# Longer load runs for q and k, 64x64 transposes and disjoint output views in an attention kernel followed by routed experts

## The chip, the cores and the metric

The kernel runs on one core of one Trainium2 chip. The metric is the device time of one execution in microseconds (us); lower is better. Before the change the median was 398.99 us (398.04 to 399.03, 3 runs). A ratio in this text is the mean time of one kernel's fast runs over the mean of the other's fast runs of the same rounds, so it is not quite the ratio of the medians quoted beside it; in the experiments the profiled execution is left out of it. A run over 1.5% above the fastest of its kernel counts as slow, and differences are read from fast runs.

## The reference

```python
# q, k, v: (8 batches, 8 heads, 576 positions, 64), float32
scores = q @ k^T / 8, blocks of 64 positions, causal by block   # row block i sees column blocks <= i
attn   = softmax(scores); x = (attn @ v) laid out as 4608 tokens x 512
# domain_id: one of 8 experts for each token; w1 (8,512,1024), w2 (8,1024,512)
for e in range(8):
    mask = domain_id == e
    out[mask] = relu(x[mask] @ w1[e]) @ w2[e]
```

A *pair* below is two heads of one batch; there are 32 pairs, four to a batch. The *routing* turns the domain ids into lists of token numbers, five blocks of 128 tokens for each expert. The experts gather their tokens' rows of x from DRAM, multiply twice, and scatter the rows of the result.

## The kernel before: the parts concerned

q, k and v come as rows of 64 elements. GpSimd's queue (POOL) casts them to 16 bit on the way, apart from batch 0, which is cast by the engines (all code below is cut and simplified):

```python
def load_sw(dst, src, t, b0, b1):            # two batches
    for c in range(5):
        nc.gpsimd.dma_start(
            out=dst[t % 2][0:n, c, o0:o1, 0:D],
            in_=src[b0:b1, :, 128*c : 128*c + n, :].rearrange("b h p d -> p (b h) d"))
```

For each pair, TensorE transposes q and k (ten transposes of 128x128), VectorE (DVE) copies them out of PSUM in one instruction, TensorE makes the scores, ScalarE (ACT) the exponentials, TensorE the product with v, and DVE normalises. The tile vS holds v in 16 bit; VE holds parts of it laid out for two heads at once, and DVE copies it from vS once a batch. One step of the routing stands between each two pairs:

```python
for p in range(npair + 1):
    emit_G(0, st)                                  # scores, first third
    if p + 2 < npair: QKs[p + 2] = emit_T(p + 2)   # transposes two pairs ahead
    emit_G(1, st); emit_P(prev); emit_G(2, st); emit_Q(prev)
    ...
    next(rout, None)                               # a step of the routing
```

The routing finds the token of each slot with 36 accumulating matmuls of one-hot tiles (`lhsT=L[:, j, :], rhs=Hh[:, :, j, :]`). In the experts every output block goes out by a scatter into one and the same tensor:

```python
osb = msb.tile([128, DM], F32, name="osb", tag="osb", bufs=4)
nc.vector.tensor_copy(out=osb[:], in_=po[:])
nc.gpsimd.indirect_dma_start(
    out=out, out_offset=bass.IndirectOffsetOnAxis(ap=tok[:, blk : blk + 1], axis=0),
    in_=osb[:], in_offset=None, bounds_check=N - 1, oob_is_err=False)
```

The softmax here doesn't subtract the row's maximum and nothing guards it: scores larger than these inputs give would overflow.

Of the kernel before, what the change touches and what calls it, by code (L numbers as in the profile page):

```python
# [8 lines left out]
F32 = mybir.dt.float32  # L9
F16 = mybir.dt.float16  # L10
# [7 lines left out]
def kernel(  # L18
# [19 lines left out]
    HP = H // 2  # L38

    ctx.enter_context(tc.manual_schedule())  # L40
    xd = nc.dram_tensor("x_rows", (N, DM), F16, kind="Internal").ap()

# [7 lines left out]
    qS = [asb.tile([128, 5, 16, D], F16, name=f"qS{i}") for i in range(2)]  # L50
    kS = [asb.tile([128, 5, 16, D], F16, name=f"kS{i}") for i in range(2)]
    vS = [asb.tile([128, 5, 16, 66], F16, name=f"vS{i}") for i in range(2)]
    VE = [asb.tile([128, 5, HP, 132], F16, name=f"VE{i}") for i in range(2)]
    ATE = [asb.tile([128, 832], F16, name=f"ATE{i}") for i in range(3)]


    def stage(nm):
        return asb.tile([128, 5, H, D], F32, name=nm, tag="stg", bufs=3)

    qf, kf, vf = stage("qf"), stage("kf"), stage("vf")  # L60
    dom_i = const.tile([128, 2 * NJ], I32, name="dom_i")

    def load_pair0(eng, dst, src):
        for h in range(2):
            eng.dma_start(
                out=dst[:, 0:4, h, :],
                in_=src[0, h, 0:512, :].rearrange("(c p) d -> p c d", p=128))
        eng.dma_start(
            out=dst[0:64, 4, 0:2, :],
            in_=src[0, 0:2, 512:576, :].rearrange("h p d -> p h d"))  # L70

    def load_rest(eng, dst, src, h0):
        for c in range(5):
            n = min(128, S - 128 * c)
            eng.dma_start(
                out=dst[0:n, c, h0:H, :],
                in_=src[0, h0:H, 128 * c : 128 * c + n, :].rearrange("h p d -> p h d"))

    load_pair0(nc.sync, qf, q)
    load_pair0(nc.scalar, kf, k)  # L80
# [3 lines left out]
    load_rest(nc.sync, qf, q, 2)  # L84
    load_rest(nc.scalar, kf, k, 2)
    load_rest(nc.sync, vf, v, 0)

    identh = const.tile([128, 128], F16, name="identh")
    make_identity(nc, identh[:])
    up = const.tile([128, 128], F16, name="up")  # L90
# [7 lines left out]
    def load_sw(dst, src, t, b0, b1):  # L98
        o0 = 8 * (b0 - 2 * t)
        o1 = o0 + 8 * (b1 - b0)  # L100
        for c in range(5):
            n = min(128, S - 128 * c)
            nc.gpsimd.dma_start(  # L103
                out=dst[t % 2][0:n, c, o0:o1, 0:D],
                in_=src[b0:b1, :, 128 * c : 128 * c + n, :].rearrange(
                    "b h p d -> p (b h) d"))

    def load_weights(w1_e, w2_e):
        w1h = wsb.tile([128, 4, Fdim], F16, name="w1h", tag="w1h", bufs=3)
        nc.gpsimd.dma_start(  # L110
            out=w1h[:], in_=w1_e.rearrange("(c p) f -> p c f", p=128))
        w2h = wsb.tile([128, 8, DM], F16, name="w2h", tag="w2h", bufs=3)
        nc.gpsimd.dma_start(
            out=w2h[:], in_=w2_e.rearrange("(c p) f -> p c f", p=128))
        return w1h, w2h

    for src, dst in ((q, qS), (k, kS), (v, vS)):
        load_sw(dst, src, 0, 1, 2)
# [5 lines left out]
    lo_f = const.tile([128, NJ], F32, name="lo_f")  # L124
# [3 lines left out]
    tok0 = const.tile([128, E * NB], I32, name="tok0")  # L128
    xg = [const.tile([128, NB, DM], F16, name=f"xg{i}") for i in range(2)]
    for i in range(2):  # L130
        nc.vector.memset(qS[i][64:128, 4], 0.0)
        nc.vector.memset(kS[i][64:128, 4], 0.0)
    nc.vector.memset(vS[0][:, :, :, 64:66], 1.0)
    for i in range(3):
        nc.vector.memset(ATE[i][:, 0:64], 1.0)
        nc.vector.memset(ATE[i][:, 64:832], 0.0)
    nc.vector.memset(VE[0][:], 0.0)

    def cast(fn, dst, src, h0, h1):
        fn(out=dst[:, 0:4, h0:h1, 0:D], in_=src[:, 0:4, h0:h1, :])  # L140
        fn(out=dst[0:64, 4, h0:h1, 0:D], in_=src[0:64, 4, h0:h1, :])

    cast(nc.vector.tensor_copy, qS[0], qf, 0, 2)
    cast(nc.scalar.copy, kS[0], kf, 0, 2)


    def onehot(L, Hh, ub, ncols, base):
        nc.vector.tensor_scalar(
            out=ub, in0=u_f[:], scalar1=base, scalar2=None, op0=ALU.subtract)
        yield  # L150
        nc.vector.tensor_tensor(
            out=Hh[:, 0], in0=iota_h[:, 0:ncols].unsqueeze(1).to_broadcast([128, NJ, ncols]),
            in1=ub.unsqueeze(2).to_broadcast([128, NJ, ncols]), op=ALU.is_equal)
        yield
        nc.vector.tensor_scalar(
            out=Hh[:, 1], in0=Hh[:, 0], scalar1=p_f[:, 0:1], scalar2=None, op0=ALU.mult)
        nc.vector.tensor_tensor(
            out=Hh[:, 2], in0=Hh[:, 0],
            in1=iota_h[:, 0:NJ].unsqueeze(2).to_broadcast([128, NJ, ncols]), op=ALU.mult)
        yield  # L160
        for j in range(NJ):
            nc.vector.tensor_scalar(
                out=L[:, j, :], in0=iota_h[:], scalar1=lo_f[:, j : j + 1],
                scalar2=None, op0=ALU.is_equal)
            if j % 4 == 3:
                yield


    def inverse(ps, L, Hh, ncols, inv, tok):
        for j in range(NJ):  # L170
            nc.tensor.matmul(
                out=ps[:, 0 : 3 * ncols].rearrange("p (a c) -> p a c", a=3),
                lhsT=L[:, j, :], rhs=Hh[:, :, j, :],
                start=(j == 0), stop=(j == NJ - 1))
        nc.vector.tensor_copy(
            out=inv, in_=ps[:, 0 : 3 * ncols].rearrange("p (a c) -> p a c", a=3))
        nc.vector.tensor_scalar(
            out=inv[:, 0], in0=inv[:, 0], scalar1=-1.0e6, scalar2=1.0e6,
            op0=ALU.mult, op1=ALU.add)
        nc.vector.tensor_tensor(out=inv[:, 1], in0=inv[:, 1], in1=inv[:, 2], op=ALU.add)  # L180
        nc.vector.tensor_tensor(out=tok, in0=inv[:, 0], in1=inv[:, 1], op=ALU.add)

    def slot_col(r_f, d_f, w, u, nm):
# [18 lines left out]
    def routing():  # L202
        nc.vector.tensor_copy(out=iota_h[:], in_=iota_i[:])
# [13 lines left out]
        ps_t = aps.tile([128, 512], F32, name="poP", tag="poP")  # L217
        ps_r = aps.tile([128, 512], F32, name="poQ", tag="poQ")
# [14 lines left out]
        cnt = asb.tile([128, E], F32, name="cnt")  # L233
# [8 lines left out]
        ri = slot_col(rank[:], dom_f[:], NJ, u_f[:], "t")  # L242
# [3 lines left out]
        nc.vector.tensor_copy(out=lo_f[:], in_=lo_i[:])  # L246
        yield

        ul = asb.tile([128, E], F32, name="ul")
        slot_col(cnt[:], iota_h[:, 0:E], E, ul[:], "e")  # L250
        yield
        um = asb.tile([128, 1], F32, name="um")
        nc.vector.tensor_reduce(out=um[:], in_=ul[:], axis=AX.X, op=ALU.max)
        umi = asb.tile([128, 1], I32, name="umi")
        nc.vector.tensor_scalar(
            out=umi[:], in0=um[:], scalar1=-float(NB * (E - 1)), scalar2=205.0,
            op0=ALU.add, op1=ALU.mult)
        nc.vector.tensor_scalar(out=n_i[:], in0=umi[0:1, :], scalar1=10, scalar2=None,
                                op0=ALU.arith_shift_right)
        nc.vector.memset(base_f[:], 0.0)  # L260
        yield
        L = asb.tile([128, NJ, 128], F16, name="L", tag="stg", bufs=3)
        Hh = asb.tile([128, 3, NJ, E * NB], F16, name="Hh", tag="stg", bufs=3)
        ub = asb.tile([128, NJ], F16, name="ub")
        yield from onehot(L, Hh, ub[:], E * NB, base_f[:, 0:1])
        ps = aps.tile([128, 512], F32, name="poP", tag="poP")
        inv = asb.tile([128, 3, E * NB], F32, name="inv")
        inverse(ps, L, Hh, E * NB, inv[:], tok0[:])
        yield
        for i in range(2):  # L270
            nc.vector.memset(xg[i][:], 0.0)
            yield


    def emit_T(p):
        b, hp = divmod(p, HP)
        t = b // 2
        PT = aps.tile([128, 2, 1024], F16, name="PT", tag="PT")
        QK = asb.tile([128, 2, 576], F16, name="QK", tag="QK", bufs=3)
        h0 = 8 * (b % 2) + 2 * hp  # L280
        for s, src in enumerate((qS[t % 2], kS[t % 2])):
            for c in range(5):
                nc.tensor.transpose(  # L283
                    out=PT[:, s, 128 * c : 128 * c + 128],
                    in_=src[:, c, h0 : h0 + 2, :].rearrange("p h d -> p (h d)"),
                    identity=identh[:])
        nc.vector.tensor_copy(out=QK[:], in_=PT[:, :, 0:576])  # L287
        return QK

# [284 lines left out]
```

## Time and profile before

| stage of the profiled run | from, to (us) | length |
|---|---|---|
| attention, to the end of the last normalisation | 0 to 161.8 | 161.8 |
| stores of x, gathers, to the first transpose of an expert | 161.8 to 169.2 | 7.4 |
| experts, to the end of TensorE's last matmul | 169.2 to 371.9 | 202.7 |
| tail, to the end | 371.9 to 398.3 | 26.4 |

The four add up to the span, so each question about the change can be put to one stage. The prediction shows the lines that say what binds each: slow loads and a late start in attention, scatters that wait for one another in the experts. Two more groups of instructions are wanted later (line, engine, operation, output and input, shapes and count, then busy us and mean ns of one):

```profile
L287 DVE COPY QK<-PT 128x1152 f16<-128x1152 f16 x32 | 23.9, 747 | 13.9 <-PE PT L283 13.5
L171 PE MATMUL poP<-Hh,L 128*128 128x120 f16 x36 | 2.9, 260 | 0.0
```

The first is the copy of q and k, once a pair. The second is the routing's 36 matmuls: 2.9 us in all, 0.08 us each (a matmul's own duration overlaps the next one's, so the busy time divided by the count is what it costs).

### The profile page before, as it was taken

The page shows a single profiled execution, that of the slowest core. Times are in us where ns is not written, and L with a number is a line of the kernel's source. Part 1 is how long each engine was busy: PE and PEld are TensorE (multiplying, and loading weights), DVE is VectorE, ACT ScalarE, POOL GpSimd, SP SyncE. Part 2 cuts the span into 40 slices and gives each one's busy share as a digit, 9 for nine tenths or more (in the row PEclk, how much of TensorE's full clock was granted, in tenths as well). Part 3 has the DMA queues.
Part 4 walks back from the last instruction along what each step waited for, and adds up shares of the span by engine and source line. Part 5 has one row for each costly group of instructions (what it writes and reads, how often), then busy time and mean ns, then how long its engine had stood idle before and what let it go on. Part 6 is the DMA issues. An engine that isn't in the chain of part 4 may idle for free. (4 is left out here: it accounts for less than half of the span.)

```text
span 398.3 us, 6825 instructions
## 1 busy us (share of the span) xinstructions
PE 274.3 (69%) x2790; PEld 174.3 (44%) x2790; DVE 150.0 (38%) x354; ACT 140.6 (35%) x197; POOL 157.5 (40%) x166
## 2 busy tenths in 40 slices
PE   0132987976887798179999986694885776799300
PEld 0121665754765576046565644353443434455100
DVE  5108899885684576121322320320320320312200
ACT  0421886867385689004141404023014004023000
POOL 9348652465253000275245145154154145122220
PEclk9999999899697899759999999699599699699955
DMA  9999999999999951232139339349139139312110
GB/s 155 181 157 156 157 177 214 186 182 183 212 157 185 195 116 63 72 100 71 53 83 195 115 98 196 129 95 222 62 78 221 72 88 205 119 65 82 45 74 14
DMA packets 134594, 52.10 MB, mean 131 GB/s; under 512 B 114202, under 2 KB 127006, under 8 KB 134560
## 3 DMA queue, kind: packets, MB, share of 16 engines
q0 software_dynamic: 115392, 43.33, 84.0%
q1 hardware_dynamic: 14432, 7.12, 8.3%
q10 hardware_dynamic: 4736, 1.18, 1.5%
q8 instruction: 23, 0.38, 0.4%
q14 instruction: 11, 0.09, 0.1%
HBM read 67.15 MB, written 15.20 MB: 207 GB/s over the span
## 5 line engine op out<-in xcount | busy, mean ns | idle before, releaser
L486 ACT ACTIVATE hT<-ph 128x640 f16<-128x640 f32 x64 | 45.0, 703 | 159.0 <-PE ph L481 159.0
L298 ACT ACTIVATE A<-ps 128x1024 f16<-128x1024 f32 (+1 forms) x96 | 82.5, 887 | 49.0 <-PE ps L293 41.7
L500 POOL DMA_INDIRECT out_dram<-osb,tok x40 | 39.7, 992 | 121.2 <-issue 81.6
L495 PE MATMUL po<-w2h,hT 128*128 128x512 f16 x320 | 76.9, 399 | 6.7 <-DVE osb L499 6.6
L499 DVE COPY osb<-po 128x512 f32<-128x512 f32 x40 | 27.7, 692 | 136.6 <-DMA out_dram<-osb,tok 109.0
L481 PE MATMUL ph<-xT,w1h 128*128 128x320 f16 x512 | 72.6, 303 | 0.2 <-DVE xT L470 0.2
L456 POOL DMA_INDIRECT xg<-x_rows,tok x40 | 40.6, 1016 | 53.6 <-issue 52.7
L481 PEld LDWEIGHTS <-w1h 128*128 128x128 f16 x512 | 50.5, 99 | 22.0 <-issue 0.6
L495 PEld LDWEIGHTS <-hT 128*128 128x128 f16 x320 | 32.5, 102 | 47.9 <-issue 15.8
L467 PE MATMUL pt<-identh,xg 128*128 128x128 f16 x160 | 18.7, 274 | 39.2 <-DMA xg<-x_rows,tok 30.3
L293 PE MATMUL ps<-QK 64*128 64x512 f16 (+3 forms) x256 | 36.7, 328 | 0.7 <-ACT ATE L298 0.7
L283 PE MATMUL PT<-identh,qS 128*128 128x128 f16 x160 | 16.5, 242 | 27.4 <-DVE QK L287 14.5
L467 PEld LDWEIGHTS <-xg 128*128 128x128 f16 x160 | 13.8, 122 | 44.3 <-DMA xg<-x_rows,tok 32.8
L350 PEld LDWEIGHTS <-A 128*128 128x128 f16 x640 | 32.0, 102 | 0.0
L470 DVE COPY xT<-pt 128x512 f16<-128x512 f16 x40 | 16.0, 421 | 35.0 <-PE pt L467 34.2
L287 DVE COPY QK<-PT 128x1152 f16<-128x1152 f16 x32 | 23.9, 747 | 13.9 <-PE PT L283 13.5
L103 POOL DMA_DIRECT2D kS<-in_k_dram x20 | 20.4, 1029 | 21.1 <-PE ps L293 10.3
L103 POOL DMA_DIRECT2D vS<-in_v_dram x20 | 20.4, 1024 | 17.0 <-DMA qS<-in_q_dram 7.2
L283 PEld LDWEIGHTS <-qS 128*128 128x128 f16 x160 | 10.9, 106 | 35.1 <-issue 21.8
L103 POOL DMA_DIRECT2D qS<-in_q_dram x20 | 21.2, 1073 | 12.3 <-PE PT L283 4.6
L283 PE MATMUL PT<-identh,kS 128*128 128x128 f16 x160 | 17.0, 240 | 9.1 <-ACT kS L140 5.1
L350 PE MATMUL poP<-vS,A 128*128 128x65 f16 x384 | 22.8, 202 | 0.0
(89 smaller groups left out, 240.1 us busy)
## 6 DMA issues: line engine op xcount, KB each, us to landing
w1h<-in_moe_w_dram POOLq DMA_DIRECT2D x8, 1024.0 KB, 8.2
w2h<-in_moe_w_dram POOLq DMA_DIRECT2D x8, 1024.0 KB, 13.5
x_rows<-x SPq DMA_DIRECT2D x8, 512.0 KB, 7.3
qS<-in_q_dram POOLq DMA_DIRECT2D x12, 256.0 KB, 19.1
kS<-in_k_dram POOLq DMA_DIRECT2D x12, 256.0 KB, 13.7
vS<-in_v_dram POOLq DMA_DIRECT2D x12, 256.0 KB, 14.0
vf<-in_v_dram SPq DMA_DIRECT2D x4, 256.0 KB, 10.7
qS<-in_q_dram POOLq DMA_DIRECT2D x7, 128.0 KB, 9.7
```

What stands on the lines that cost most here:

```text
L103: nc.gpsimd.dma_start(out=dst[t % 2][0:n, c, o0:o1, 0:D], in_=src[b0:b1, :, 128 * c : 128 * c + n, :].rearrange("b h p d -> p (b h) d"))
L283: nc.tensor.transpose(out=PT[:, s, 128 * c : 128 * c + 128], in_=src[:, c, h0 : h0 + 2, :].rearrange("p h d -> p (h d)"), identity=identh[:])
L293: nc.tensor.matmul(out=o[:, i], lhsT=QK[h, 1, 128 * c : 128 * c + 128], rhs=QK[h, 0, 128 * c + 64 : 576], start=True, stop=True)
L298: nc.scalar.activation(out=o, in_=i, func=AF.Exp, scale=0.125)
L350: nc.tensor.matmul(out=po[:, off + 66 * i : off + 66 * i + 65], lhsT=at_block(st, i, c, m), rhs=vt[:, c, h0 + i, 0:65], start=False, stop= ...
L456: nc.gpsimd.indirect_dma_start(out=g[:, blk, :], out_offset=None, in_=xd, in_offset=bass.IndirectOffsetOnAxis(ap=tok[:, blk : blk + 1], ax ...
L467: nc.tensor.transpose(out=pt[:, dc], in_=g[:, blk, 128 * dc : 128 * dc + 128], identity=identh[:])
L481: nc.tensor.matmul(out=ph[:, i, 0:hw], lhsT=w1h[:, dc, 128 * fc : 128 * fc + 128], rhs=xT[:, dc, hw * i : hw * i + hw], start=(dc == 0), s ...
L486: nc.scalar.activation(out=hT[:, fc].rearrange("p (i n) -> p i n", i=2), in_=ph[:, :, 0:hw], func=AF.Relu)
L495: nc.tensor.matmul(out=po[:], lhsT=hT[:, fc, 128 * blk : 128 * blk + 128], rhs=w2h[:, fc, :], start=(fc == 0), stop=(fc == 7))
L499: nc.vector.tensor_copy(out=osb[:], in_=po[:])
L500: nc.gpsimd.indirect_dma_start(out=out, out_offset=bass.IndirectOffsetOnAxis(ap=tok[:, blk : blk + 1], axis=0), in_=osb[:], in_offset=None ...
```

## The change

Its intent: fetch q and k in long runs, let DVE do less fixed work, and let the scatters go out without waiting for one another. The core of the diff, with cuts, and some lines put in words:

```diff
+    outs = dram_disjoint_views(out, E * NB)
...
-    qS/kS/vS tiles, batch 0 by row loads on SyncE and ScalarE, cast by engines
+    def load_qk(g0, g1):                 # nine positions a partition, two batches a tile
+        for src, dst in ((q, qh), (k, kh)):
+            for i in range(2):
+                nc.gpsimd.dma_start(
+                    out=dst[t % 2][64*i : 64*i + 64, o : o + g1 - g0, :],
+                    in_=src.rearrange("b (g i) (p j) d -> i p (b g) (j d)", i=2, j=9)[i, :, g0:g1, :])
+    load_qk(0, 1)
+    nc.gpsimd.memset(vst[0][:, :, 0, 0:1], 0.0)     # holds batch 0's v back
+    load_qk(1, HP)
+    for c in range(5): nc.sync.dma_start(out=vst[0][0:n, c], in_=v[0, ...])
+    load_qk(HP, 2 * HP)
...
-            for c in range(5): transpose 128x128          # per q and per k
-        nc.vector.tensor_copy(out=QK[:], in_=PT[:, :, 0:576])
+            for j in range(9):
+                for i in range(2): transpose 64x64        # per q and per k
+            nc.vector.tensor_copy(
+                out=QK[:, s].rearrange("p (n j) -> p n j", j=9),
+                in_=PT[:].rearrange("p j n -> p n j"))
...
-    two PSUM tiles for the product, two normalisations and reciprocals a pair
+    one PSUM tile, one normalisation and one reciprocal a pair
-            L [128, NJ, 128], Hh [128, 3, NJ, ncols]      # one-hot tiles
+            L [128, 128, NH], Hh [128, 3, ncols, NH]      # in two halves, j innermost
-                lhsT=L[:, j, :], rhs=Hh[:, :, j, :]
+                lhsT=L[:, :, j], rhs=Hh[:, :, :, j]
-    value casts: casting loads
+    value casts: cast_v on POOL (batch 0 on DVE)
...
+            if nxt is not None and blk + 1 < NB:
+                transpose_block(*nxt, blk + 1)            # next expert's, between output blocks
-            osb = msb.tile(..., bufs=4)
+            osb = msb.tile(..., bufs=6)
-                out=out,
+                out=dst[blk],                             # one of 40 disjoint views
+            for f in todo[2*blk : 2*blk + 2]: f()         # weights in 256 KB pieces
```

## The prediction

> **What bounds the kernel now.** I read the busy line and the slices, then waits, timeline and windows stage by stage, because the busy shares hide two quite different stages.
>
> ```profile
> PE 274.3 (69%) x2790; PEld 174.3 (44%) x2790; DVE 150.0 (38%) x354; ACT 140.6 (35%) x197; POOL 157.5 (40%) x166
> PE   0132987976887798179999986694885776799300
> DMA  9999999999999951232139339349139139312110
> GB/s 155 181 157 156 157 177 214 186 182 183 212 157 185 195 116 63 72 100 71 53 83 195 115 98 196 129 95 222 62 78 221 72 88 205 119 65 82 45 74 14
> ```
>
> Attention is the first 16 slices (0 to 161 us), the experts the rest. In attention the DMA engines sit at 9 for 14 slices (140 us), much of it at a flat 156 GB/s: that plateau is the casting loads, whose packets are 256 B read and 128 B written (GB/s counts the written side, so 312 GB/s are read). The compute engines are not full meanwhile:
>
> ```profile
> 0.00:10.00 10.00, 0.71 (x5) 0.45 (x5) 5.22 (x14) 0.00 (x0) 9.20 (x19) 1.00 1.16 155
> 30.00:40.00 10.00, 2.56 (x16) 1.43 (x18) 8.61 (x18) 1.02 (x1) 8.65 (x9) 1.00 2.34 156
> 100.00:120.00 20.00, 17.80 (x285) 13.70 (x284) 15.29 (x39) 11.94 (x17) 8.43 (x8) 0.83 2.00 183
> 140.00:160.00 20.00, 18.60 (x355) 13.21 (x353) 13.82 (x34) 18.46 (x27) 0.00 (x0) 0.98 0.32 83
> ```
>
> Columns: window, length, then PE, weight loads, DVE, ACT, POOL busy with counts, clock, DMA, GB/s. Once the loads are over (140 to 160) ACT is busy 18.46 of 20 us, and in the timeline the first score matmul of a pair starts at 144.74, 147.67, 150.61, 153.55: 2.94 us a pair. That is the ACT floor; 32 pairs cost 94 us. Attention takes 161, because pair 0 starts at 20.6 us, pair 1 only at 38 us (value cast and vS wait for slow loads), and the middle waits for loads.
>
> In the experts TensorE needs 8.86 us for 64 first-layer matmuls and 7.07 us for 32 of the second (0.221 each, 8.84 for 40). Eight experts are 142 us, plus transposes. But from 175.5 to 371.9 us pass 196 us. The waits name it:
>
> ```profile
> DVE osb L499 <- DMA out_dram<-osb,tok: 109.0, 23, 14.2
> POOL out_dram L500 <- DMA out_dram<-osb,tok: 25.8, 10, 3.1
> PE pt L467 <- DMA xg<-x_rows,tok: 30.3, 9, 8.5
> ...
> 380.78 0.98 POOL L500 DMA_INDIRECT out_dram<-osb,tok  x1 [3.07 <-DMA out_dram<-osb,tok]
> 384.23 0.98 POOL L500 DMA_INDIRECT out_dram<-osb,tok  x1 [2.48 <-DMA out_dram<-osb,tok]
> 387.69 0.98 POOL L500 DMA_INDIRECT out_dram<-osb,tok  x1 [2.48 <-DMA out_dram<-osb,tok]
> ```
>
> Every scatter waits until the one before has landed, one per 3.45 us; gathers stand behind them in the same queue, and TensorE waits for gathers. After its last matmul (371.9) the chain still has scatters to work off until 387.7, and the end comes 10.6 us after that.
>
> [...] flat 312 GB/s read with 256 B packets against slices at 222 GB/s written, over 400 read if they were weights alone. [...] 1152 elements in 747 ns and 512 in 421 make 0.51 ns each plus about 160. [...] The nearest is a reduction in SBUF that steps 144 bytes, 674 ns for 288 elements where contiguous operations of that size take 453. [...] after the wait at 250 us second-layer matmuls stand 0.43 us apart instead of 0.221.
>
> **The change, part by part.**
>
> *Loads.* q and k come as runs of nine positions (2304 B): 8192 of them in place of 73,728 packets of 256 B. 18.9 MB at an estimated 400 GB/s are 47 us, v at the old 312 is 30, two experts' weights (8.4 MB; three before) 21, the x stores about 12: 110 us of DMA in all, no longer the bound but not idle. Pair 0 needs four small loads, issued at about 1 us each: scores at 9 us, not 20.6. Pair 1's q and k land near 14, v near 15; its cast and VE end near 19, so the rhythm starts at 19 instead of 38.
>
> *TensorE in attention.* 36 transposes of 64x64 replace 10 of 128x128 a pair. Twelve 64x64 score matmuls pass in 0.38 us, so I take 28 ns each: 1.0 against 0.66 us. TensorE was busy 2.5 of 2.94 us, now 2.8: just under ACT.
>
> *DVE in attention.* The q and k copies now read PSUM with step 64[...]: 576 elements at 1.04 ns plus 155 are 0.755 us, twice, against one of 0.747. One normalisation of 768 elements (958, from 558 at 384 and 425 at 256 elements) and one reciprocal (226) replace 1.35 us by 1.18. The VE copies stay 1.65 us a batch, 0.4 a pair. Sum 3.1 us, slightly less with overlap of neighbouring copies: at ACT's level. The routing (20 us before; about 16 now, as its one-hot tiles get contiguous inner runs and fewer operations) is spread over the first 17 pairs, one microsecond each. From 19 us DVE has 30 x 1.45 + 32 x 1.1 + 7 x 1.6 + 16 = 106 us of work. So attention is DVE-bound and ends near 130 us (161 before). The single po tile adds a wait for the normalisation, which the next scores and transposes (2 us) cover. Value casts move to POOL, some 3 us a batch, beside all this.
>
> *Between the stages.* Last normalisation to first expert transpose was 161.8 to 169.2; the store of only 128 columns on two queues saves perhaps 0.3. The first expert split into halves starts after three gathered blocks: 14 us from first transpose to the end of its first layer, against 16.3.
>
> *Experts.* Disjoint views remove the wait of scatter on scatter, six output tiles replace four, transposes of the next expert sit between output blocks (1.4 us an expert). 14 + 7 x 8.86 + 8 x 8.84 + 7 x 1.4 = 156.5 us. Does POOL keep pace? Gathers and scatters pass at 1.31 us in the trace; eight weight pieces an expert at an estimated 0.75: 5 x 1.31 + 5 x 1.31 + 6 = 19.1 us against TensorE's 19.1. A backlog from the start (10 gathers, 8 pieces, 5 gathers: 25 us) reaches the fifth expert with the six tiles just enough, and then weights end. The DMA, with about 4 MB written per 19 us (210 GB/s), is near its best slices. I add 4 us for stalls.
>
> *Tail.* Last matmul, copy 0.7, scatter, and the same 10.6 us: 11.5 instead of 26.4.
>
> Sum: 130 + 7.3 + 156.5 + 4 + 11.5 = 309 us.
>
> **Rivals.**
> 1. *The strided PSUM copy pays[...].* If it costs 1.75 times per element, as that reduction hints, it takes 1.2 us; DVE gets 0.9 us more a pair, 27 us in all, attention ends near 155 and the total is about 333. For: [...]the reduction; against: the reduction has groups of eight that could cost by themselves. I hold it for nearly as likely as the plain sum.
> 2. *POOL becomes the bound of the experts.* With pieces at 1.1 us (the 256 KB loads' 1140 ns) the backlog grows by 3 us an expert for five experts, and the output tiles fill: 8 to 12 us more, 319. For: 231 DMA issues instead of 156, plus casts; against: the 1 MB weight loads needed only 814 and 941 ns.
> 3. *The loads still bind attention.* Pair 8 needs 11.8 MB, near 35 us[...]. A few microseconds, mostly under DVE's time.
> 4. *DVE overlaps well and ACT sets 2.94 us:* attention to 122, total about 300.
>
> **Range and chances.** Between 309 and 333 with rival 1 near even, I predict 318. Good overlap on one side, strided reads together with a POOL backlog on the other give 298 to 342. Faster by over 2% is near certain: the scatter chain and the late start alone are 40 us of waits whose causes are gone. Slower would need something like a PSUM read several times slower than any here.
>
> **What would show it.** Right: scores of pair 1 by 20 us; attention's end at 125 to 157; DVE over 90% busy and ACT with gaps in the first half of attention; QK copies of 0.75 us (sum) or 1.2 us (rival 1); scatters no longer waiting on scatters; dense TensorE with clock near 1.0 in the experts; under 13 us from the last matmul to the end. Wrong: QK copies far off both values, strided weight reads that stretch the first layer beyond 8.9 us, output copies that still wait long for scatters, or DMA at 9 throughout attention.

The paragraph on readings comes from the trace before: "the nearest" means the nearest reading to a DVE copy that reads PSUM with a step, of which there was none; around the wait that ended at 250.13 us the granted clock stood at 1.00 up to 249, at 0.50 from 251 to 257 and at 1.00 again from there. The 1.04 ns an element of the q and k copies fits the normalisations there (558 ns for 384 elements, 425 for 256); that a copy with a step of 64 would fall to that rate from its 0.51 ns was the author's estimate, and so was a weight piece at 0.75 us (the readings were 814 and 941 ns for 1 MB, 1140 for 256 KB).

## More of the kernel before

Runs fell on several chips. Where the kernel before took about 406 us and not 399, only ratios and readings inside one trace are compared, and a control of the changed kernel was run on such a chip.

## The result

The changed kernel takes 340.28 us (median of 4 fast runs, 339.04 to 342.2) against 399.01 us in the same rounds. The ratio is 0.8535, 95% interval 0.8489 to 0.858: faster by 14.7%. The profiled run has a span of 337.3 us.

| stage | before | after | predicted |
|---|---|---|---|
| attention | 161.8 | 163.1 | 130 |
| to the first transpose | 7.4 | 7.2 | 7.3 |
| experts | 202.7 | 153.3 | 160.5 |
| tail | 26.4 | 13.7 | 11.5 |
| sum | 398.3 | 337.3 | 309 (hedged to 318) |

All of the gain lies in the experts and the tail. The attention, for which most of the diff was written, won nothing. The page of the profile, first TensorE's busy time, then tenths in 40 slices (of 8.4 us here):

```profile
PE 274.4 (81%) x3622; PEld 179.6 (53%) x3622; DVE 154.0 (46%) x294; ACT 140.6 (42%) x201; POOL 198.6 (59%) x263
...
PE   2404968798989999797169999999999999999930
PEclk9999995978767899989559999999999999999995
DMA  6999968993899759912337999896989999402020
```

Slices 22 to 38, the experts, are solid 9 for TensorE; before, that stretch was a sequence of 5 to 9. In the first 20 slices the DMA is no longer at 9 throughout, and still TensorE has holes, and its granted clock (PEclk, in tenths of full speed) falls to half in places. The table of windows says it more sharply (window, length, PE, weight loads, DVE, ACT, POOL, then clock, DMA share and GB/s):

```profile
84.00:88.00 4.00, 4.00 (x62) 2.46 (x60) 1.70 (x3) 2.05 (x2) 2.00 (x3) 0.50 0.50 126
...
200.00:220.00 20.00, 20.00 (x138) 12.41 (x136) 5.20 (x10) 6.81 (x10) 13.47 (x17) 1.00 0.93 202
```

Both windows show TensorE fully busy, but the first one, in attention and right after the first 18 of the routing's matmuls, at half clock; the clock fell from 1.00 to 0.50 while those 18 ran, from 80.4 to 84.5 us, and again while the other 18 ran, from 102.7 to 106.8, though TensorE counts as busy in them (4.07 and 4.10 of 4.1 us). It also fell after a plain wait, one of 1.43 us that ended at 65.35: it stood at 1.00 up to 67.5 and at 0.50 from 68.0 to 71.0. What that did to one and the same pair of score matmuls, before and after that wait, stands in the timeline (start, duration):

```profile
63.53 0.39 PE L310 MATMUL ps<-QK 64*128 64x512 f16 x2
69.28 0.61 PE L310 MATMUL ps<-QK 64*128 64x512 f16 x2
```

So this stall was paid twice, once as idle time and once as a slow pair after it: 3.7 us from 69.3, 2.99 undisturbed.

The scatters, in the timeline of POOL:

```profile
321.12 0.98 POOL L540 DMA_INDIRECT out_dram<-osb,tok  x1 [0.75 <-DVE osb L539]
322.84 0.98 POOL L540 DMA_INDIRECT out_dram<-osb,tok  x1 [0.74 <-DVE osb L539]
```

They leave 1.73 us apart, each released by its own copy; before, it was 3.45 us, each held by the scatter before it. TensorE has no wait in the experts from 200 to 320 us.

**Where attention's time goes.** I took the start of each pair's first score matmul from the timeline. Undisturbed pairs follow each other after 2.99 us (2.94 before). What came in place of that:

```
changed kernel, starts of pairs 0 to 31 (us):
7.7 16.9 34.3 37.3 40.5 43.5 50.7 56.9 60.2 63.5 69.3 73.0 76.3 84.5 89.0 91.9
98.4 106.7 111.6 114.8 117.8 121.7 124.7 127.7 130.7 133.7 137.5 141.9 146.2 149.2 152.6 155.6
```

From pair 2 on, 29 periods take 121.3 us; 29 undisturbed ones are 86.7. Pair 2 starts at 34.3 and not near 22; from there on the pairs follow one another, and below this is called the start of the rhythm. The reason for the late start is in the waits of the first 36 us (who waited for what: us in total, times, longest):

```profile
PE PT L298 <- DVE QK L302: 12.7, 1, 12.7
DVE vS L114 <- DMA vst<-in_v_dram: 10.8, 2, 9.5
```

DVE's cast of batch 0's v waits until 27.1 us for the load, and the copies of pair 2's q and k stand behind it on the same engine, so that TensorE waits with it. That load goes through SyncE's queue in 256-byte packets beside the long runs of q and k. A memset on its tile that stands in POOL's queue lets it go only at 4.4 us (1.3 without it, in experiment 4); after that it takes a median of 15.6 us to land.

The groups of instructions in attention settle what each new operation costs:

```profile
L302 DVE COPY QK<-PT 128x576 f16<-128x576 f16 x64 | 45.4, 748 | 8.7 <-PE PT L298 8.4
L383 DVE TENSOR_TENSOR x<-po,rc 128x768 f16<-128x768 f32 x32 | 30.6, 957 | 1.1
...
L196 PE MATMUL PT<-Hh,L 128*128 128x120 f16 x36 | 8.2, 398 | 0.9 <-DVE QK L302 0.9
```

The copy out of PSUM with step 64 takes 748 ns for 576 elements: after the fixed 155 ns of the prediction that is 1.03 ns an element, as in its plain sum, and my first rival (1.2 us) is wrong. The normalisation is as predicted. What I had not looked at is the last line: the same 36 routing matmuls cost 8.2 us and no longer 2.9. They now read both operands with a step of 36 bytes.

Two more things show in the trace. First, DVE and POOL hold each other up: the operations of both take longer here than elsewhere. In this stretch POOL writes four descriptors, then casts a batch of v:

```profile
88.69 3.07 POOL L104 DMA_DIRECT2D vst<-in_v_dram  x4
90.87 1.07 DVE L180 TENSOR_SCALAR Hh<-Hh,p_f 128x720 f16<-128x720 f16 x1
91.70 2.97 POOL L114 CAST vS<-vst 128x1024 f16<-128x1024 f32 x3
91.86 1.35 DVE L183 TENSOR_TENSOR Hh<-Hh,iota_h 128x720 f16<-128x720 f16 x1
93.93 0.47 PE L298 MATMUL PT<-identh,qh 64*64 64x64 f16 x18 [1.60 <-DVE QK L302]
```

The two DVE operations take 0.41 and 0.53 us where POOL is quiet (experiment 2), and POOL's three casts 2.58 us at 75.35, 106.56 and 121.74, not 2.97. The pair's copies come late and TensorE waits 1.60 us. The first DVE operation ends with the descriptors (91.94 against 91.76); by what means, the trace does not show. Below this is called the hold-up. Second, TensorE has gaps that the profile calls "issue", with nothing waited for: 0.81 us at 120.6 and 1.33 at 141.8, 512 matmuls apart, in the time of the weight loads (issued from 112.8 to 134.7, landing some 8 us later).

The theories put to the test: **A**, the late v and the stalls by routing steps, with half clock after each, cost the 33 us; **D**, the loads bind attention whatever is done; **V**, DVE's amount of work binds (98 of the 129 us from 34.3 to 163.1; 18.77 of 20 from 60 to 80). Theories F, L and others came up on the way.

### The profile page after: what moved, and what is told of

Read it like the earlier page. It is cut to its first block, busy times and chain, and to the rows that moved or that the text cites. A ratio compares the mean times of both kernels' runs of the same rounds, so it can differ in the third digit from the quotient of the medians.

```text
span 337.3 us, 8495 instructions
## 1 busy us (share of the span) xinstructions
PE 274.4 (81%) x3622; PEld 179.6 (53%) x3622; DVE 154.0 (46%) x294; ACT 140.6 (42%) x201; POOL 198.6 (59%) x263
## 5 line engine op out<-in xcount | busy, mean ns | idle before, releaser
L522 ACT ACTIVATE hT<-ph 128x640 f16<-128x640 f32 (+1 forms) x72 | 46.4, 645 | 110.0 <-PE ph L516 94.2
L104 POOL DMA_DIRECT2D vst<-in_v_dram x56 | 42.3, 766 | 25.1 <-DMA kh<-in_k_dram 17.9
L302 DVE COPY QK<-PT 128x576 f16<-128x576 f16 x64 | 45.4, 748 | 8.7 <-PE PT L298 8.4
L366 PE MATMUL po<-vS,A 128*128 128x65 f16 x640 | 38.5, 205 | 0.8 <-issue 0.8
L361 PE MATMUL po<-VE,ATE 128*128 128x130 f16 x160 | 34.2, 239 | 4.8 <-DVE x L383 2.9
L298 PE MATMUL PT<-identh,qh 64*64 64x64 f16 x576 | 17.5, 208 | 24.7 <-DVE QK L302 16.2
L298 PEld LDWEIGHTS <-qh 64*64 64x64 f16 x576 | 14.2, 121 | 33.4 <-issue 24.3
L383 DVE TENSOR_TENSOR x<-po,rc 128x768 f16<-128x768 f32 x32 | 30.6, 957 | 1.1
L114 POOL CAST vS<-vst 128x1024 f16<-128x1024 f32 (+1 forms) x21 | 18.8, 928 | 9.0 <-PE po L366 6.8
L361 PEld LDWEIGHTS <-ATE 128*128 128x128 f16 x160 | 16.3, 102 | 10.1 <-issue 8.0
## 6 DMA issues: line engine op xcount, KB each, us to landing
vst<-in_v_dram SPq DMA_DIRECT2D x4, 256.0 KB, 15.6
```

What stands on the lines that cost most here:

```text
L104: nc.gpsimd.dma_start(out=vst[b % 3][:, 0:4, h, :], in_=v[b, h, 0:512, :].rearrange("(c p) d -> p c d", p=128))
L298: nc.tensor.transpose(out=PT[h, j], in_=src[h, g, 64 * j : 64 * j + 64], identity=identh[h, h])
L302: nc.vector.tensor_copy(out=QK[:, s].rearrange("p (n j) -> p n j", j=9), in_=PT[:].rearrange("p j n -> p n j"))
L361: nc.tensor.matmul(out=o[:, 1:131], lhsT=st["AE"][:, 128 * m : 128 * m + 128], rhs=VE[b % 2][:, m, hp, 1:131], start=True, stop=(m == 0))
L366: nc.tensor.matmul(out=o[:, 1 + 65 * i : 66 + 65 * i], lhsT=at_block(st, i, c, m), rhs=vS[b % 3][:, c, hp, 1 + 65 * i : 66 + 65 * i], star ...
L522: nc.scalar.activation(out=hT[:, fc].rearrange("p (i n) -> p i n", i=2)[:, i0:i1], in_=ph[:, i0:i1, 0:hw], func=AF.Relu)
```

## The experiments

"Attention's end" is the end of the last normalisation in the profiled run.

**1. Routing after the last pair.**

```diff
-        if p:
-            next(rout, None)          # the rest then runs after the loop
```

> The changed kernel with the routing taken out of the pair loop and done in one piece after the last pair. Attention's end is read as the end of the last normalisation (163.1 us in the changed kernel); nothing but the routing's place is changed. Theory A (each routing step between pairs stalls TensorE, and TensorE then runs at half clock for several us, so that pairs take 4.5 to 7 us and not 3.0): from the start of the rhythm at 34 us the pairs pass at 3.0 to 3.2 us, attention ends at 130 to 138 us; the routing then stands alone for some 20 us, so that the total is only 325 to 338. Rival D (the loads bind attention; DMA stands at 0.8 to 0.9 until 140 us): attention still ends at 155 to 163 and the total rises to 355 or more. Rival V (VectorE's amount of work binds: it was busy 98 of 129 us): 17 us of work go, attention ends near 146, total near 343.

Measured: attention's end at 142.4 us, the 29 periods 101.0 us; ratio 0.8605, 349.39 us on a chip where before takes 406.5. Rival D's 155 is refuted. The routing inside the loop costs attention 20 us (121.3 to 101.0, and this run was even on a slower chip), more than its 17 us of DVE time. The total did not fall: the routing then stands alone, and the gap before the experts grows from 7.2 to 28.0 us. The 142.4 lies between theory V's 146 and theory A's 138, and 17 of the 20 us are DVE's work itself, so this run does not part the two. And 14 us beyond undisturbed pairs are left, with no routing in between. The three largest of the remaining gaps, in TensorE's timeline:

```profile
66.87 0.28 PE L366 MATMUL po<-vS,A 128*128 128x65 f16 x4 [1.46 <-issue]
95.10 0.22 PE L361 MATMUL po<-VE,ATE 128*128 128x130 f16 x1 [1.38 <-issue]
123.05 0.19 PE L298 MATMUL PT<-identh,kh 64*64 64x64 f16 x1 [1.93 <-issue]
```

No engine is named. Counted with the windows view, the matmuls from one gap to the next, with those of 0.90 us at 45.7 and 1.02 at 74.2, are 512, 128, 512 and 640: multiples of 128. (By hand I had found 124, 504 and 639, as the next expectation says.) Among the DMA queues of the changed kernel are two for instructions; this is the larger (packets, MB, share):

```profile
q8 instruction: 29, 0.48, 0.5%
```

TensorE has 3622 matmuls and as many weight loads; 7244 instructions in 29 packets are 250 a packet, 125 matmuls, near the 128 between the gaps. (Before: 5580 instructions, 23 packets, 243 a packet.) That this queue carries TensorE's instructions is inferred from these counts; no view names its engine. Hence theory F: TensorE waits for its own instructions, which stand behind the loads.

**2. No loads after the second batch** (wrong result).

```diff
-        if p: next(rout, None)                       # as in experiment 1
-                if b % 2 == 0: load_qk(HP * b, HP * b + 2 * HP)
-                load_v(b, 0, 4)
                 cast_v(fn, b - 1)                    # reads batch 1's tile from now on
-                load_v(b, 4, H)
-        if p == 4 * B - 12: ...                      # weights of the first two experts,
+    for e in range(2): ...                           # now after the loop
```

> Wrong result on purpose: as the run with the routing last, and in addition nothing is loaded after batch 1's v and the first two batches' q and k (later batches compute on the old tiles; the value casts on POOL and the stores of x stay; the first two experts' weights are loaded after the last pair). So from about 40 us on the DMA is almost idle. In the run with the routing last, 29 pair periods took 101.0 us against 87 undisturbed, and the gaps in TensorE's stream named 'issue' (0.90, 1.46, 1.02, 1.38, 1.93 us) stood 124, 504 and 639 matmuls apart, multiples of about 126. Theory F (what is left are waits of TensorE for its own instructions, which come by DMA in blocks of some 128 matmuls with their weight loads and stand behind the loads): without loads there is no such gap over 0.5 us, pairs pass at 3.0 us throughout, the last normalisation ends at 130 to 134 us. Rival C (what is left comes from the casts on POOL and the in-order VectorE): it still ends at 139 or later and the gaps stay. The total says nothing here.

Measured: attention's end at 135.9 us. One thing went otherwise than planned: POOL had nothing left to wait for, ran ahead, and issued the weights at 96 us, before the last pairs. So this one kernel shows both conditions. Two windows (columns as above):

```profile
60.00:80.00 20.00, 19.66 (x541) 14.74 (x539) 17.52 (x29) 18.55 (x27) 2.58 (x3) 1.00 0.17 52
...
100.00:120.00 20.00, 15.80 (x421) 11.47 (x423) 14.07 (x24) 14.68 (x22) 4.87 (x9) 1.00 1.12 214
```

And every gap of over 0.9 us in TensorE's stream between 36 and 120 us:

```profile
104.72 0.41 PE L298 MATMUL PT<-identh,kh 64*64 64x64 f16 x14 [0.94 <-issue]
111.19 0.22 PE L361 MATMUL po<-VE,ATE 128*128 128x130 f16 x1 [1.58 <-issue]
117.38 0.19 PE L298 MATMUL PT<-identh,kh 64*64 64x64 f16 x1 [1.68 <-issue]
```

From 40 to 97 us, with the DMA almost idle, pairs take 2.99, 2.99, 2.99 and 3.48 us in turn (the fourth holds the VE copies) and there is no such gap. Once the weights flow, gaps come 128 and 128 matmuls apart. Theory F fits: the instruction queue is only 0.5% of the DMA, and between 36 and 120 us the gaps of over 0.9 us come only once the weights have been issued, at 96. (The trace doesn't show the time of a single fetch; that fetches are late then is inferred from the spacing of the gaps and from the two conditions.) The casts stayed on POOL, so rival C is refuted for the gaps.

The clean stretch also shows how close the three engines are: of 20 us, PE is busy 19.66, ACT 18.55, DVE 17.52. There is no slack to take up a microsecond of anything. The fullest is TensorE: from 36 to 97 us it waits 1.7 us in all, while DVE and ACT wait for it (6.4 and 5.2 us). I had predicted that DVE binds; in these undisturbed pairs it does not, TensorE does.

**3. Routing at the beginning.**

```diff
         if p == 0:
             QKs[2] = emit_T(2)
+            for _ in rout: pass
+            cast_v(nc.vector.tensor_copy, 0); emit_VE(0)      # moved here
```

> The changed kernel with the whole routing done by VectorE and TensorE at the beginning, after the transposes of pair 2 and ahead of the value cast of batch 0, in the time in which both wait for batch 0's v (9.5 us of idle VectorE to 27 us). Theory A: the rhythm starts some 4 us later (at 36 to 40 us and not 34), but the pairs then pass at 3.0 to 3.2 us; attention ends at 132 to 142, total 310 to 322 us. Rival D (loads bind): attention's end stays within 5 us of 163, total 335 to 345. Rival V (amount of VectorE work): only the part that fills the wait is won, about 9 us, total near 331.

Measured: 346.33 us, ratio 0.8527, the changed kernel's own; attention's end at 161.1. Theory A's and V's gains are both absent. The total is about what rival D gave, but its reason is not the trace's. The routing could not use the idle time well, because it waits for itself:

```profile
28.84 4.14 PE L196 MATMUL PT<-Hh,L 128*128 128x120 f16 x18 [7.92 <-DVE L L188]
```

A second such block starts at 36.77. DVE stands still for 4.24 us during each of them, the value cast comes at 41.9 us and pair 2 at 47.7, not at 36 to 40. After that, 29 periods take 106.7 us with six issue gaps of 1.05 to 2.27 us among them.

**4. Batch 0's v first.**

```diff
-    nc.gpsimd.memset(vst[0][:, :, 0, 0:1], 0.0)               # v no longer held
-    load_qk(HP, 2 * HP)
+    nc.gpsimd.tensor_copy(out=hold[0:64], in_=vst[0][0:64, :, 0, 0])   # waits for v
+    load_qk(HP, 2 * HP)
```

> The changed kernel with batch 0's v issued at once, and the q and k of pairs 4 to 7 held on POOL until it has landed. Routing stays between the pairs. Theory A's second part (the late v of batch 0 delays the rhythm by some 13 us): v lands near 14 us and not 27, the rhythm starts at 20 to 24 us, attention ends 8 to 13 us earlier than 163, total 328 to 334 us, with the stalls in the middle unchanged. Rival D: what v gains, q and k lose; the middle waits longer for loads and the total stays within 4 us of 340.

Measured: 341.7 us on a chip where before takes 406.5, ratio 0.8397; the control (experiment 8) has 0.8563 on another such chip, so 2% is won, 6.7 us, give or take 3: between theory A's 8 to 13 and rival D's 4 at most, and not clear of either. The profiled run was slow (347.75 us), so I take only the order of events from it. The rhythm starts at 24.4 us, nearly as theory A said, 10 us earlier. But then DVE runs into the next load:

```profile
35.98 1.09 DVE L393 COPY VE<-vS 64x1280 f16<-64x1280 f16 x2 [3.43 <-POOL vS L115]
```

Batch 1's v is not cast yet. In that slow run two pair periods grew to 11.5 and 11.8 us. By the ratio of the fast runs a good part of the head start remained; some of it went as rival D says, "what v gains, q and k lose", though here it was the next v.

**5. Weights of the one-hot matmul with unit step.**

```diff
-            L = sb.tile([128, 128, NH], ...)      lhsT=L[:, :, j]
+            L = sb.tile([128, NH, 128], ...)      lhsT=L[:, j]
+            # DVE writes it through a view with j innermost, a step of 256 B
```

> The changed kernel with the routing's one-hot tile L, which TensorE loads as weights, laid out with unit step for TensorE (VectorE writes it with a step of 256 B instead); the moving tile keeps its step of 36 B. If the weight's step is what makes the 36 matmuls of the inverse cost 8.2 us (0.228 each, against 0.08 each in the kernel before, where both are contiguous), they fall to about 3 us; if it is the moving side's step, they stay at 8 us and only the weight loads shorten. VectorE's writes to L may slow from 754 ns. The time as a whole: within 4 us of 340 in either case.

Measured: 365.13 us (one run, where before takes 406.5). The two groups:

```profile
L188 DVE TENSOR_TENSOR L<-iota_x,lo_h 128x1152 f16<-128x1152 f16 x4 | 21.1, 5279 | 0.1
L196 PE MATMUL PT<-Hh,L 128*128 128x120 f16 x36 | 8.1, 394 | 9.0 <-DVE QK L302 9.0
```

The matmuls still cost 8.1 us, so it is not the weight's step. Writing L with a step of 256 B takes DVE 5279 ns in place of 754, seven times as long. The expected total, within 4 us of 340, missed for that reason: attention's end moved to 182.2.

**6. The moving operand with unit step.**

```diff
-            Hh = sb.tile([128, 3, ncols, NH], ...)      rhs=Hh[:, :, :, j]
+            Hh = sb.tile([128, NH, 3, ncols], ...)      rhs=Hh[:, j]
+            # DVE's small operands broadcast along the innermost axis; all writes with unit step
```

> The changed kernel with only the routing's moving one-hot tile laid out with unit step for TensorE (VectorE writes it with unit step too and takes its small operands by broadcast). If the moving side's step of 36 B is what makes these 36 matmuls cost 0.228 us each, they fall to 0.08 to 0.1 us, 3 to 4 us in all against 8.2; the two pairs concerned get 2.5 us shorter each, and with fewer half-clock stretches the total falls by 5 to 9 us, to 331 to 336 on a chip where the changed kernel takes 340 (ratio 0.83 to 0.845). If the step is not the cause, nothing moves (ratio 0.8535 as before).

Measured: 337.41 us, ratio 0.8449 (0.8416 to 0.8483). The matmuls:

```profile
L196 PE MATMUL PT<-Hh,L 128*128 128x120 f16 x36 | 2.6, 226 | 0.3 <-DVE QK L302 0.3
```

That settles it: 0.07 us each against 0.228, by the moving side's step alone. It also shows the clock without that step. The window that stood at 0.50 in the changed kernel:

```profile
84.00:88.00 4.00, 3.67 (x85) 2.86 (x84) 3.83 (x8) 2.42 (x4) 0.45 (x1) 1.00 0.02 4
```

The two pairs that follow the routing's matmuls take 3.12 and 3.05 us here, 4.48 and 4.86 in the changed kernel. The total moved by 1%: the time is a little above what was expected (331 to 336), the ratio just inside. In the profiled run attention's end is at 162.1. One issue gap of 2.68 us and longer one-hot operations (the third takes 1.83 us on average, 0.93 before) probably took most of the gain back; no run tested that.

**7. The kernel before with the disjoint views alone.**

```diff
+    outs = dram_disjoint_views(out, E * NB)
-                out=out,
+                out=dst[blk],
```

> The kernel before with the disjoint output views alone: every scatter goes to its own view, everything else as before. If the wait of scatter on scatter was what held the experts, no scatter waits for one any more, TensorE waits for gathers only briefly; experts take 157 to 168 us and not 202.7, the tail from the last matmul 12 to 15 us and not 26.4; total 340 to 352, so that nearly the whole gain of the change (61 of 399 us) is there. If six output tiles, interleaved transposes and the loads in pieces are needed as well, the experts stay above 180 us and the total above 365.

Measured: 343.09 us against 400.02, ratio 0.8599: 57 of the change's 59 us by this edit alone. One of its scatters, in POOL's timeline:

```profile
327.74 0.98 POOL L502 DMA_INDIRECT out_dram<-osb,tok  x1 [0.75 <-DVE osb L501]
```

Attention ends at 161.0, the experts take 160.2 us and the tail 12.3.

**8. The control: the changed kernel again**, on the chip of experiments 9, 11 and 12.

> The changed kernel once more, unaltered, as the control on the chip of the next three runs. Ratio to the kernel before 0.849 to 0.858, 338 to 342 us on a chip where before takes 399; attention's end within 2 us of 163.

Measured: ratio 0.8563, 350.29 us against 406.46; attention's end at 167.1 and the experts 160.3 us. The time expected for a 399-us chip does not apply, and attention's end is 4 us later and not within 2. TensorE's rate is the same on this chip (64 first-layer matmuls in 8.86 us), but it has short waits in the experts, some for the output copies.

**9. The changed kernel with one output view.**

```diff
-    outs = dram_disjoint_views(out, E * NB)
+    outs = [out] * (E * NB)
```

> The changed kernel with one view of the output for all scatters, everything else as changed. If the disjoint views alone carry the gain in the experts (as the kernel before with views showed, ratio 0.86), every scatter waits again for the one before, and the weight pieces and gathers of the next experts stand behind it on POOL: attention ends at 163 as before, the experts take 195 to 225 us, total 385 to 415. If six output tiles, weights in pieces and interleaved transposes hide that wait, the experts stay under 175 us and the total under 365.

Measured: 390.86 us, ratio 0.9509 (two fast runs, 384.2 and 389.05); against the control's 0.8563 that is 9.5 points of the time before, 38 us. The longest wait of the output copies (the profiled run was a slow one):

```profile
DVE osb L539 <- DMA out_dram<-osb,tok: 52.3, 18, 6.3
```

The chain is back. The experts take 182.7 us and the tail 34.8 in this run, so the other changes (six tiles, weights in pieces, interleaved transposes) hide part of the wait: the experts lie between the 195 I expected and the rival's 175, in a slow run that may overstate them. The total, well above the rival's 365, decides.

**10. Four mendings at once.** Batch 0's v first; five routing steps before pair 1's transposes; the moving one-hot tile with unit step; VE copies one pair later.

```diff
+            for _ in range(5): next(rout)           # p == 0, before QKs[1] = emit_T(1)
-        if p < npair and hp == 3 and b + 1 < B: emit_VE(b + 1)
+        if 0 < p < npair and hp == 0: emit_VE(b)
```

> A version meant to beat both: batch 0's v first as in the run of that name; the first five routing steps before pair 1's transposes, where VectorE waits for q and k; the moving one-hot tile with unit step; the copies into VE of the next batch one pair later, so that VectorE does not wait for POOL's cast (3.4 us of wait there in the run with v first). Theory A (stalls, each followed by half clock, and the late v are what costs): the rhythm starts near 25 us, attention ends at 138 to 146, total 316 to 326 on a chip where the changed kernel takes 340 (ratio 0.79 to 0.82). Rival D (loads bind the middle): what starts early waits later, attention's end stays above 155, ratio above 0.835.

Measured: 330.71 us against 400.02, ratio 0.8301 (0.8246 to 0.8357); the profiled run, the fastest, took 324.65. (Beside it two of the three others, 332.31 and 332.87, are slow; the ratio takes these three, so the trace is of a quicker run than the ratio.) The rhythm starts at 24.2, attention ends at 148.9: between theory A's 146 and rival D's 155. What holds pair 7:

```profile
45.90 0.68 PE L299 MATMUL PT<-identh,kh 64*64 64x64 f16 x17 [4.10 <-DMA kh<-in_k_dram]
```

That is a load, the k of pair 8. It comes in one transfer with seven other pairs' k.

**11. The same, with two things mended:** q and k of later batches one batch at a time, and only batch 1's VE copies put off.

```diff
-                    load_qk(HP * b, HP * b + 2 * HP)
+                    load_qk(HP * b, HP * b + HP)            # the second half after load_v(b, 4, H)
```

> The version of before (v first, early routing steps, unit-step moving one-hot tile) with two things mended that its trace showed: TensorE waited 4.1 us for the k of pair 8, which was loaded with seven other pairs' q and k in one transfer of 576 KB, so q and k of later batches come one batch at a time; and TensorE waited 8.9 us in 7 places for VE copies that stood too late, so that only batch 1's are put off. Theory A: the wait for k falls below 1 us, those for VE to near 0, attention ends at 136 to 143 (148.9 in the version of before), ratio 0.79 to 0.82 against before. Rival D (the total of bytes up to 45 us binds, 11.5 MB read): the wait moves to another load, attention's end at 147 or later, ratio 0.825 to 0.835.

Measured: ratio 0.8208 (0.817 to 0.8247), 334.59 us where before takes 406.46. The waits for k and for VE are gone as theory A said, but attention's end at 150.0 is what rival D expected. That end decides little, though: on this chip the control's is 4 us later than the first run's, and the ratio, 1.1% below experiment 10's, is at the edge of theory A's 0.82. The trace shows neither's reason for what is left. It shows the hold-up, in a fast run:

```profile
72.71 3.30 DVE L209 TENSOR_TENSOR tok<-inv 128x40 int32<-128x40 f32 x1
73.29 2.66 POOL L115 CAST vS<-vst 128x1024 f16<-128x1024 f32 x3
...
86.75 3.74 DVE L393 COPY VE<-vS 64x1280 f16<-64x1280 f16 x2
86.83 2.67 POOL L115 CAST vS<-vst 128x1024 f16<-128x1024 f32 x3
```

An operation on 40 elements, 0.20 us elsewhere, takes 3.30 and ends with three casts of POOL in a row; two VE copies take 3.74 us in place of 0.99. TensorE waits 2.66 us for the copies behind the first. Pairs 15 and 18 start 7.55 and 7.33 us after the ones before them.

**12. v of batches 1 to 7 by SyncE.**

```diff
     def load_v(b, h0, h1):
-            nc.gpsimd.dma_start(...)
+            nc.sync.dma_start(...)
```

> As the run before this one, with v of batches 1 to 7 issued by SyncE and not by POOL. Theory L (POOL's descriptor work and VectorE shut each other out: small int32 operations took 1.89 and 2.03 us in place of 0.41 and 0.18 while POOL issued four loads and cast): with 63 issues of 0.75 us off POOL, VectorE's operations keep their short durations, POOL's casts come earlier, attention ends 3 to 8 us earlier than in the run before this one. Rival H (SyncE's queue moves 256-byte packets slowly beside POOL's transfers: batch 0's v took 15.6 us to land): v arrives late, VectorE waits for casts, attention's end the same or up to 20 us later.

Measured: 329.76 us where before takes 406.46 and the control 350.29; ratio 0.8067 (0.8008 to 0.8126). Attention ends at 142.0, 8.0 us earlier than in experiment 11: theory L. The value loads land after a median of 6.4 us, so rival H is refuted. DVE's operations keep their size:

```profile
L393 DVE COPY VE<-vS 64x1280 f16<-64x1280 f16 x14 | 7.7, 549 | 0.1
```

In experiment 11 the mean was 699 ns; for the one-hot L it was 1361 there and 875 here. From the rhythm's start to attention's end the same 163 DVE operations are busy for 93.3 us, 100.8 in experiment 11: nearly all of the 8 us. (The edit also makes POOL's casts come earlier; this run does not part that from the hold-up.) This version beats both kernels: its fast runs average 328.36 us and the control's 348.85 on the same chip, 5.9% less.

## Why the prediction was right or wrong

The time fell inside the range (298 to 342), near its upper end, and that is in part luck. The upper end stood for strided reads together with a backlog on POOL, and neither came; the time got there because attention ended 33 us later than the sum had it. Of the signs named, the scatters came true, while attention's end (163.1, not 125 to 157) and the tail (13.7, not under 13) did not. The mechanism of the gain was right, that of the attention was wrong. By its steps:

- **Experts: right, and the larger part.** The wait of scatter on scatter was the bound, and disjoint views remove it (experiments 7 and 9, from both sides). 153.3 us came, 160.5 was predicted: the 4 us for stalls were not needed, and an output block with its transposes starts 1.95 us after the last one, 1.73 without, so that transposes cost 5 x 0.22 = 1.1 us an expert. (The 0.221 us of a second-layer matmul counts the end of the last one in; blocks 1.73 us apart make 0.216.) Only the start, to the end of the first layer, was longer: 15.6 us, 14 predicted. On the control's chip the experts took 160.3.
- **What carries the gain: not weighed.** The prediction listed views, tiles, pieces and interleaving together. Alone, the views give 57 us; all the rest of the change without them gives 5% (0.9509); together 59. They overlap, since each hides the same wait.
- **Rival 1, the strided PSUM copy, nearly even in my chances: wrong.** 748 ns measured, 755 in the plain sum. (Its own 27 us would have made 157 and 336, not 155 and 333.) The 9 us added for it hid part of the error elsewhere. With the step the copy takes 1.03 ns an element; the contiguous copy of the kernel before took 0.51 (1152 elements in 747 ns). That is shown for this read of PSUM and for no other copy.
- **Rival 2, POOL's backlog: did not come.** A weight piece occupies POOL for 580 ns (w1) and 564 (w2), below even the 0.75 us assumed.
- **"The rhythm starts at 19": failed.** The prediction means pair 1, with its v ready, so pair 2 near 22. Pair 2 started at 34.3, which is 12 of the 33 us missing in attention. The prediction had v "near 15" from bytes over bandwidth; but the load of v goes in small packets beside long runs, and landed at 27. With v first the rhythm starts at 24.2 to 24.4 (experiments 4 and 10), so 10 of the 12 are the late v.
- **"So attention is DVE-bound and ends near 130": failed, the other 21 us** (128.8 us from pair 2's start to the end, in place of 108). DVE's cost of a pair was about right: 2.9 us predicted, 2.7 busy in the clean stretch of experiment 2. But there TensorE, not DVE, is the fullest, and pairs take 2.99, each fourth 3.48. DVE was over 90% busy, the sign I had named, only from 60 to 80 us; from pair 2's start to the end it was 76%. The error was to add up one engine's work where three engines are nearly full, and to let the rest be "beside". The undisturbed pairs account for 2 of the 21 us (2.99 us for 2.9). Routing, counted as 16 us of DVE time, costs 20 (experiment 1). After it 14 us remain. What the runs show in them are gaps of TensorE while loads are under way (0.94 to 1.68 us in experiment 2; theory F) and DVE held up beside POOL's work (3.30 us for 0.20 in experiment 11; 100.8 us busy for 93.3 between experiments 11 and 12). I can't split the 14 us exactly.
- **The routing's matmuls: missed.** The prediction counted the gain of contiguous runs for DVE ("fewer operations") and not what the same layout does to TensorE: 8.2 us for 2.9, and half clock after them. Experiment 6 shows that it is the moving operand.
- **Rival 3, "mostly under DVE's time": half right.** Loads do bind, but as late v (27.1 us), late k (4.10 us of wait in experiment 10) and, by theory F, late instructions rather than by the sum of bytes.
- **The gap between the stages: right**, 7.2 against 7.3. **Tail:** mis-sized, 13.7 against 11.5; from the last scatter's issue to the end it is 12.7 us, 10.6 before. Experiment 12 has 16.0 there. Why is not settled; no run was aimed at it.

Half clock after waits is read from the clock in the windows and from the durations. Only for the routing's matmuls did a run take its cause away, together with their own cost (experiment 6). No run kept the waits and held the clock up, so their share is not separately shown.

## What to carry to other kernels

When writes to one tensor don't overlap, say so to the scheduler first; here that edit was worth more than all the rest of a large change. Where several engines are nearly full in a loop (here TensorE 98%, ACT 93%, DVE 88% in experiment 2), don't add up one engine's work: look for what makes any of them wait, and count small things (here a step of 36 bytes in a moving operand, 0.228 us a matmul for 0.07; POOL's descriptors and casts beside DVE, 1.07 us for 0.41; gaps of up to 1.68 us in TensorE's stream while loads flow). When a layout is changed for one engine, check what the other engines that read it pay.
